# Attention and two mixture layers on one core: narrow matmuls in uninterrupted runs, and four buffers moved

## The chip, the core and the metric

The kernel runs on one core of a Trainium2 chip. The core has a matrix engine (TensorE, PE in the profile), three engines for elementwise work (VectorE or DVE, ScalarE or ACT, GpSimd or POOL) and SyncE (SP), which issues nearly all DMA transfers of this program, strictly in its own order. Every engine takes its instructions in the order in which they were written down when the program was built, and waits for other engines by semaphores. TensorE writes to PSUM, which has eight banks of 128 partitions. The metric is device time in microseconds (us).

## What is computed

```
attention: q, k, v of (4 batches, 8 heads, 576 tokens, 64)
    out_d  = softmax(mean4(q) @ mean4(k).T / 8) @ mean4(v)   # 144 tokens, each repeated 4 times
    out_l  = softmax over |i - j| < 4 of (q @ k.T / 8) @ v
    x      = (out_d + out_l) as (2304 tokens, 512)
first layer:  x = ((x @ w1) * (x @ w2)) @ w3 @ w_out         # w1, w2: 512x1024, w3: 1024x1024, w_out: 1024x512
second layer, 8 experts:
    e   = argmax(x @ w_gate);  p = softmax(x @ w_gate)[e]
    out = p * sigmoid((x @ w_output_gate)[e]) * (relu(x @ w1[e]) @ w2[e])
```

The weights of the first layer come as 64-bit floats; the kernel turns their bits into 32-bit ones with integer instructions on VectorE.

## The kernel before

A product of full precision is made of three matmuls (`mm3`, L390 to L392): each operand is split into a rounded part and a remainder, and high*high, high*low and low*high are summed in one PSUM bank. These are the wide matmuls: their output covers all 128 partitions, and they have 256, 272 or 384 columns here.

Order of the work. (1) Gate stage: for each eighth of `w_out`, `gate_step` loads it, converts it (`f64_bits`, L122, three VectorE instructions L127 to L129 through a PSUM bank), transposes it on TensorE (L318), copies the bank out on ScalarE (L320) and multiplies by the gate weights (L322). (2) w3 stage: `w3_part` converts w3 in 16 pieces, and `wc_half` makes the 16 halves of `wc` = w3 @ [w_out, gates] with 24 wide matmuls each (tile `w3T`), which `wc_out` brings to SBUF. (3) For each of six groups of 384 tokens (g = 0 to 5): the product stage `g1_step`, eight steps of 24 wide matmuls for (x @ w1) * (x @ w2), then `g2_step` with `wc` (tile `h`). In group 0, `w_parts` converts w1 and w2 beside the product stage, 16 pieces. (4) The experts, from about 482 us on; the change does not touch them.

Attention is laid beside (2) and (3). It has 16 units (a pair of heads of one batch), each with five steps that `step()` deals out by a table: `a_T`; `a_S1` with 24 local score matmuls (L191, output on 32 partitions, four of them side by side in the array) and three score matmuls on the means (L202); `a_S2`; `a_V1` with six transposes (L245); `a_V2` with 4 matmuls (L256) and 12 matmuls (L260), outputs on 64 partitions. L191, L256 and L260 are called narrow here. One record of the trace counts such a matmul twice ("x48" are 24 matmuls). Their banks are the three of the tag `at`.

What sets the order: the building tool orders each engine's list by priority, which is the place in the code; a step's instructions are raised by 120 places (`tc.high_priority(offset=120)`), and an instruction is taken once it is expected to be ready. Loads and buffers: a unit's `kz` (L160), `kc` (L153) and `v4` (L164) have one buffer each, so the next unit's load is issued when the last reader of the one before is done; the load of w1 and w2 pieces (tile `f`, L119, four buffers) is issued by `ahead()`. PSUM before: two banks `g1` (pool `ps1`), two `g2` (pool `ps2`), three `at`, one for conversions (`cv`, pool `psc`).

An uninterrupted run of narrow matmuls between wide ones is called an island below.

Of the kernel before, what the change touches and what calls it, by code (L numbers as in the profile page):

```python
# [20 lines left out]
P = 128  # L21
# [27 lines left out]
def attention_moe_kernel(ctx: ExitStack, tc: tile.TileContext, q, k, vw_in, v4_in, w1, w2, w3, w_out,  # L49
# [7 lines left out]
    psa = actx.enter_context(tc.tile_pool(name="psa", bufs=3, space=PSUM))  # L57
    psc = actx.enter_context(tc.tile_pool(name="psc", bufs=1, space=PSUM))
# [44 lines left out]
    staged = {}  # L103

# [3 lines left out]
    def f64_load(m, n):  # L108
        if m == "o":
            t = mt([P, 512], I64, "f64w", tag=f"W{n}")  # L110
            src = w_out[P * n:P * n + P, :]
        elif m == "3":
            t = mt([P, 512], I64, "f64w", tag=f"W{8 + n % 4}")
            src = w3[n]
        else:
            t = mt([P, 512], I64, "f64", tag=f"W{3 + 4 * m}") if n % 2 and n < 6 else mt([P, 512], I64, "f64", bufs=2)
            src = (w1, w2)[m][n]
        for c in pieces(m, n):
            nc.sync.dma_start(out=t[:, c], in_=src[:, c])  # L119
        staged[m, n] = t  # L120

    def f64_bits(t, dst):  # L122
        w = t.bitcast(U32).rearrange("p (n t) -> p n t", t=2)
        lo, hi = w[:, :, 0], w[:, :, 1]

        c = psc.tile([P, 512], F32, name="cv", tag="cv").bitcast(U32)[:, 0:dst.shape[-1]]
        nc.vector.tensor_scalar(c, hi, 3, 0x3FFFFFF8, op0=ALU.logical_shift_left, op1=ALU.bitwise_and)  # L127
        nc.vector.scalar_tensor_tensor(c, hi, 0xC0000000, c, op0=ALU.bitwise_and, op1=ALU.bitwise_or)
        nc.vector.scalar_tensor_tensor(dst, lo, 29, c, op0=ALU.logical_shift_right, op1=ALU.bitwise_or)  # L129
# [17 lines left out]
    st = {}  # L147

# [35 lines left out]
    def a_S1(u):  # L184
# [4 lines left out]
        for g in range(24):  # L189
            b, j = divmod(g, 4)  # L190
            nc.tensor.matmul(sl[32 * j:32 * j + 32, b], qT[:, 24 * g:24 * g + 32], kz[:, :, 24 * g:24 * g + 32],  # L191
                             start=True, stop=True, tile_position=(0, 32 * j))
# [8 lines left out]
        for qb in range(3):  # L201
            nc.tensor.matmul(sd[:, qb], qf[:, 96 * qb:96 * qb + 96], d["kd"], start=True, stop=True)  # L202
# [30 lines left out]
    def a_V1(u):  # L233
# [8 lines left out]
        for kb in range(2):  # L242
            pv = psa.tile([P, 512], F32, name="at", tag="at")
            for qb in range(3):
                nc.tensor.transpose(pv[0:72, 96 * qb:96 * qb + 96], ed[:, qb, 72 * kb:72 * kb + 72], ident[0:96, 0:96])  # L245
# [3 lines left out]
    def a_V2(u):  # L249
# [4 lines left out]
        for kb in range(2):  # L254
            for h in range(2):
                nc.tensor.matmul(xl[0][64 * h:64 * h + 64, 288:432], vd[:, kb, h, :], pt[:, kb, 144 * h:144 * h + 144],  # L256
                                 start=(kb == 0), stop=(kb == 1))
        for c in range(6):
            for h in range(2):
                nc.tensor.matmul(xl[c // 3][64 * h:64 * h + 64, 96 * (c % 3):96 * (c % 3) + 96], vw[:, c, D * h:D * h + D],  # L260
                                 bd[:, 2 * c + h, :], start=True, stop=True)
# [45 lines left out]
    def gate_step(f, gps, src):  # L307
        t = mt([P, DM], F32, "wf", tag=f"W{12 + f % 4}")
        for c in pieces("o", f):
            f64_bits(src[:, c], t[:, c].bitcast(U32))  # L310
# [26 lines left out]
    def w3_part(i, hf, w3T, src, wf3):  # L337
        t = wf3[:, (2 * i + hf) % 3, :]
        f64_bits(src, t.bitcast(U32))
# [19 lines left out]
    def w_part(m, f):  # L359
# [5 lines left out]
        f64_bits(src, t.bitcast(U32))  # L365
# [510 lines left out]
    for n in range(KF):  # L876
        if n == 1:
            nc.sync.dma_start(out=wg[:, :, 0:E], in_=w_gate.rearrange("(k p) e -> p k e", p=P))
            nc.sync.dma_start(out=wg[:, :, E:2 * E], in_=w_ogate.rearrange("(k p) e -> p k e", p=P))
# [26 lines left out]
    for i in range(KF):  # L906
        if i == KF - 2:
            ahead()
# [137 lines left out]
def _laid_out(inputs):  # L1046
# [18 lines left out]
    for n in ("moe_w1", "moe_w2"):  # L1065
        a[n] = _np.asarray(a[n]).reshape(KD, P, KF, P).transpose(2, 1, 0, 3).reshape(KF, P, 512)
    w = _np.asarray(a["moe2_w1"])
# [30 lines left out]
```

## Time and profile before

| what | value |
|---|---|
| median of 3 runs | 777.54 us (775.76 to 778.25) |
| the profiled execution's own time | 771.75 us |
| its span (first to last instruction) | 769.9 us |
| TensorE busy | 739.4 us, 96% of the span |
| VectorE busy | 436.3 us, 57% |
| ScalarE busy | 279.6 us, 36% |
| GpSimd busy | 322.9 us, 42% |
| mean granted TensorE clock | 0.989 of full speed |

Start times in a timeline are more telling than durations: matmuls overlap in the engine, so what one costs is the distance from its start to the next one's. Stages by the trace: gate stage to 28.67 us, w3 stage to 116.26 us, the product stage of group 0 to 168.06 us, and from there groups 0 to 5 until 482 us.

### The profile page before, as it was taken

Reading aid. Unit: us, or ns where it says so; the run is one execution under the profiler, and the core shown is the slowest. Engines: PE = TensorE matmul, PEld = TensorE weight load, DVE = VectorE, ACT = ScalarE, POOL = GpSimd, SP = SyncE. Lnnn points to the kernel's source line nnn. Section 1 sums busy time; section 2 is a strip of 40 time slices with the busy share of each in tenths; the row PEclk is TensorE's granted clock in tenths of the full one; section 3 lists DMA queues with packets and bytes.
Section 4 is the critical chain, followed back from the end, with each engine's and each line's share of the span. In section 5 each row is a group of like instructions: output and inputs, shape, how many; then the busy total and the mean of one; then the engine's idle time right before and its main releaser. Section 6 shows DMA issues by size and latency. Waiting matters only on the chain.

```text
span 769.9 us, 14699 instructions
## 1 busy us (share of the span) xinstructions
PE 739.4 (96%) x5710; PEld 683.3 (89%) x5711; DVE 436.3 (57%) x940; ACT 279.6 (36%) x624; POOL 322.9 (42%) x306
## 2 busy tenths in 40 slices
PE   5789999999999999999999999989999999999995
PEld 3667987888978898899899999978999999999994
DVE  8977897962653254445324343455765566676731
ACT  3423534550233223323421212045443644544610
POOL 6744576852360125213201112035654656755611
PEclk9899999999999999999999999998999999999999
DMA  9994565542131313121110010256645447447301
GB/s 325 332 240 139 173 189 160 171 136 91 54 109 31 115 29 111 47 77 38 42 42 22 1 42 1 60 199 241 213 146 210 148 149 268 146 148 260 111 23 39
DMA packets 38264, 97.72 MB, mean 127 GB/s; under 512 B 6018, under 2 KB 12930, under 8 KB 38192
## 3 DMA queue, kind: packets, MB, share of 16 engines
q1 hardware_dynamic: 34768, 86.82, 35.1%
q0 software_dynamic: 3424, 9.93, 3.6%
q8 instruction: 46, 0.75, 0.4%
q14 instruction: 26, 0.21, 0.1%
HBM read 84.93 MB, written 12.29 MB: 126 GB/s over the span
## 4 chain that ended last, share of the span: by engine, by line
PE 86%; issue 5%; POOL 3%; DVE 3%; DMA 1%; ACT 1%; SPq 0%; POOLq 0%; ACTq 0%
PE g L390 24%; PE g L392 24%; PE g L391 23%; PE at L260 3%; PE at L191 3%; PE at L256 2%; PE at L202 2%; PE tr L686 1%; PE at L245 1%; PE tr L779 1%; POOL out_dram L769 1%; DMA early<-in_moe_w_dram 1%; PE g L322 1%; POOL W L713 1%; DVE wf L129 1%
## 5 line engine op out<-in xcount | busy, mean ns | idle before, releaser
L390 PE MATMUL g<-xh,W 128*128 128x384 f32 x384 | 133.8, 349 | 0.0
L392 PE MATMUL g<-xh,W 128*128 128x384 f32 x384 | 131.0, 342 | 0.0
L391 PE MATMUL g<-xl,W 128*128 128x384 f32 x384 | 130.8, 341 | 0.0
L713 DVE TENSOR_TENSOR W<-raw,W 128x1024 fp32r<-128x1024 f32 x32 | 87.9, 2780 | 32.2 <-ACT W L711 30.1
L713 POOL TENSOR_TENSOR W<-raw,W 128x1024 fp32r<-128x1024 f32 x29 | 82.8, 2879 | 37.0 <-ACT W L711 37.0
L390 PE MATMUL g<-xT,W 128*128 128x288 f32 (+6 forms) x256 | 82.2, 321 | 1.0 <-ACT xT L690 1.0
L391 PE MATMUL g<-xT,W 128*128 128x288 f32 (+6 forms) x256 | 80.2, 313 | 0.0
L392 PE MATMUL g<-xT,W 128*128 128x288 f32 (+6 forms) x256 | 80.0, 312 | 0.0
L423 POOL TENSOR_TENSOR h<-a,h 128x384 fp32r<-128x384 f32 x30 | 30.7, 1023 | 113.9 <-ACT h L421 113.7
L390 PEld LDWEIGHTS g<-xh,W 128*128 128x128 f32 x384 | 72.2, 188 | 3.2 <-issue 0.4
L392 PEld LDWEIGHTS g<-xh,W 128*128 128x128 f32 x384 | 72.1, 188 | 1.9 <-issue 0.4
L391 PEld LDWEIGHTS g<-xl,W 128*128 128x128 f32 x384 | 72.2, 188 | 1.5 <-issue 0.2
L390 PE MATMUL g<-wc,h 128*128 128x272 f32 (+1 forms) x240 | 70.2, 293 | 0.0
L391 PE MATMUL g<-wc,h 128*128 128x272 f32 (+1 forms) x240 | 70.0, 292 | 0.0
L390 PE MATMUL g<-h,W 128*128 128x288 f32 (+5 forms) x224 | 70.0, 312 | 0.0
L392 PE MATMUL g<-wc,h 128*128 128x272 f32 (+1 forms) x240 | 69.9, 292 | 0.0
L391 PE MATMUL g<-h,W 128*128 128x288 f32 (+5 forms) x224 | 68.1, 304 | 0.0
L392 PE MATMUL g<-h,W 128*128 128x288 f32 (+5 forms) x224 | 68.1, 304 | 0.0
L711 ACT CAST W<-raw 128x1024 fp32r<-128x1024 f32 x61 | 59.8, 1046 | 8.1 <-DMA raw<-in_moe_w_dram 4.3
L419 DVE TENSOR_TENSOR a<-g,a 128x384 f32<-128x384 f32 x48 | 26.7, 556 | 60.2 <-PE g L392 56.4
L739 ACT ACTIVATE h<-g 128x288 fp32r<-128x288 f32 (+6 forms) x64 | 27.9, 436 | 78.6 <-PE g L392 76.3
L390 PEld LDWEIGHTS g<-xT,W 128*128 128x128 f32 x256 | 49.1, 192 | 1.5 <-ACT xT L690 1.4
(255 smaller groups left out, 1721.8 us busy)
## 6 DMA issues: line engine op xcount, KB each, us to landing
raw<-in_moe_w_dram SPq DMA_DIRECT2D x61, 512.0 KB, 3.6
f64w<-in_moe_w_dram SPq DMA_DIRECT2D x16, 512.0 KB
f<-in_moe_w_dram SPq DMA_DIRECT2D x16, 512.0 KB, 6.5
vw<-in_vw_dram SPq DMA_DIRECT2D x16, 384.0 KB, 3.2
kc<-in_k_dram SPq DMA_DIRECT2D x16, 288.0 KB, 6.4
qT<-in_q_dram SPq DMA_DIRECT2D x16, 288.0 KB, 4.3
kz<-in_k_dram SPq DMA_DIRECT2D x32, 144.0 KB, 3.7
v<-in_v_dram SPq DMA_DIRECT2D x16, 288.0 KB
```

What stands on the lines that cost most here:

```text
L191: nc.tensor.matmul(sl[32 * j:32 * j + 32, b], qT[:, 24 * g:24 * g + 32], kz[:, :, 24 * g:24 * g + 32], start=True, stop=True, tile_positio ...
L202: nc.tensor.matmul(sd[:, qb], qf[:, 96 * qb:96 * qb + 96], d["kd"], start=True, stop=True)
L256: nc.tensor.matmul(xl[0][64 * h:64 * h + 64, 288:432], vd[:, kb, h, :], pt[:, kb, 144 * h:144 * h + 144], start=(kb == 0), stop=(kb == 1))
L260: nc.tensor.matmul(xl[c // 3][64 * h:64 * h + 64, 96 * (c % 3):96 * (c % 3) + 96], vw[:, c, D * h:D * h + D], bd[:, 2 * c + h, :], start=T ...
L390: nc.tensor.matmul(ps, whi, xhi, start=first, stop=False)
L391: nc.tensor.matmul(ps, whi, xlo, start=False, stop=False)
L392: return nc.tensor.matmul(ps, wlo, xhi, start=False, stop=last)
L419: nc.vector.tensor_tensor(a, pp[1][:, 0:G], a, op=ALU.mult)
L423: eng.tensor_tensor(lo, a, hi.bitcast(F32), op=ALU.subtract)
L711: nc.scalar.copy(out=hi, in_=t)
L713: ins = eng.tensor_tensor(lo, t, hi.bitcast(F32), op=ALU.subtract)
L739: return nc.scalar.activation(out=t[:, 0, 0:C], in_=ps[:, 0:C], func=AF.Relu), nc.vector.scalar_tensor_tensor(t[:, 1, 0:C], ps[:, 0:C], 0. ...
```

## The change

The 24 matmuls of L191, the three of L202, each three of L245, and the 16 of L256 and L260 are each raised by 600 places (`burst`). The conversion bank is given up: `f64_bits` takes a `g1` bank in the gate and w3 stages and a `g2` bank for w1 and w2, and `at` has four banks in place of three. The first loads of w1 and w2 are queued on SyncE behind the last load of w3. The two gate weights are laid out on the host so that each partition's part is contiguous in DRAM. Lines after 145 stand some 4 to 8 lines further down in the changed file: L191 is L196, L245 is L252, L256 is L264, L260 is L268, L390 to L392 are L398 to L400.

```diff
-    psa = actx.enter_context(tc.tile_pool(name="psa", bufs=3, space=PSUM))
-    psc = actx.enter_context(tc.tile_pool(name="psc", bufs=1, space=PSUM))
+    psa = actx.enter_context(tc.tile_pool(name="psa", bufs=4, space=PSUM))
...
-            nc.sync.dma_start(out=t[:, c], in_=src[:, c])
+            f64_last[0] = nc.sync.dma_start(out=t[:, c], in_=src[:, c])
...
-    def f64_bits(t, dst):
+    def f64_bits(t, dst, ps, tag):
...
-        c = psc.tile([P, 512], F32, name="cv", tag="cv").bitcast(U32)[:, 0:dst.shape[-1]]
+        c = ps.tile([P, 512], F32, name=tag, tag=tag).bitcast(U32)[:, 0:dst.shape[-1]]
...
+    def burst():
+
+        return tc.high_priority(offset=600)
...
-        for g in range(24):
-            b, j = divmod(g, 4)
-            nc.tensor.matmul(sl[32 * j:32 * j + 32, b], qT[:, 24 * g:24 * g + 32], kz[:, :, 24 * g:24 * g + 32],
-                             start=True, stop=True, tile_position=(0, 32 * j))
+        with burst():
+            for g in range(24):
+                b, j = divmod(g, 4)
+                nc.tensor.matmul(sl[32 * j:32 * j + 32, b], qT[:, 24 * g:24 * g + 32], kz[:, :, 24 * g:24 * g + 32],
+                                 start=True, stop=True, tile_position=(0, 32 * j))
...
-            f64_bits(src[:, c], t[:, c].bitcast(U32))
+            f64_bits(src[:, c], t[:, c].bitcast(U32), ps1, "g1")
...
-        f64_bits(src, t.bitcast(U32))
+        f64_bits(src, t.bitcast(U32), ps1, "g1")
...
-        f64_bits(src, t.bitcast(U32))
+        f64_bits(src, t.bitcast(U32), ps2, "g2")
...
-            nc.sync.dma_start(out=wg[:, :, 0:E], in_=w_gate.rearrange("(k p) e -> p k e", p=P))
+            nc.sync.dma_start(out=wg[:, :, 0:E], in_=w_gate.rearrange("p (k e) -> p k e", e=E))
...
-            ahead()
+            with tc.issue_after(f64_last[0].ins):
+                ahead()
...
+    for n in ("moe2_w_gate", "moe2_w_output_gate"):
+        a[n] = _np.asarray(a[n]).reshape(KD, P, E).transpose(1, 0, 2).reshape(P, KD * E)
```

TensorE's order in the w3 stage before, where the second matmuls of the first unit meet a half of `wc` (`g_672`):

```order
L256 MATMUL at<-pt,vd 64x144
L390 MATMUL g_672<-wo,w3T 128x256
L256 MATMUL at<-pt,vd 64x144
L391 MATMUL g_672<-wc,w3T 128x256
L260 MATMUL at<-bd,vw 64x96
L392 MATMUL g_672<-wo,w3T 128x256
L260 MATMUL at<-bd,vw 64x96
L390 MATMUL g_672<-wo,w3T 128x256
```

The change, in the same stage, from one half of `wc` (`g_797`) to the next (`g_824`):

```order
L398 MATMUL g_797<-wo,w3T 128x256
L399 MATMUL g_797<-wc,w3T 128x256
L400 MATMUL g_797<-wo,w3T 128x256
L268 MATMUL at<-bd,vw 64x96 x12
L196 MATMUL at<-kz,qT_109 32x64 x3
L208 MATMUL at<-kd,qz 96x144
L196 MATMUL at<-kz,qT_109 32x64
L208 MATMUL at<-kd,qz 96x144
L196 MATMUL at<-kz,qT_109 32x64
L208 MATMUL at<-kd,qz 96x144
L196 MATMUL at<-kz,qT_109 32x64 x19
L398 MATMUL g_824<-wo,w3T 128x272
```

The twelve matmuls with `bd` now stand in one row between wide ones; the 24 with `kz` still share their place with three of the means, which are wide.

TensorE's order at the end of the gate stage and the start of the w3 stage before (`g_384`: last transposes of the gates; `g_442`, `g_469`: the first two halves of `wc`):

```order
L202 MATMUL at<-kd,qz 96x144 x2
L318 MATMUL g_324<-ident,wf 128x128 x4
L322 MATMUL g_161<-wot,wg 32x128 x8
L330 MATMUL g_384<-ident,gs 128x128 x2
L390 MATMUL g_442<-wo,w3T 128x256
L391 MATMUL g_442<-wc,w3T 128x256
L390 MATMUL g_469<-wo,w3T 128x272
L391 MATMUL g_469<-wo,w3T 128x272
L392 MATMUL g_442<-wo,w3T 128x256
```

The same place in the change (`g_381`, `g_439`, `g_466` are the same three; `qT_110` and `qT_109` belong to the second and the third unit):

```order
L196 MATMUL at<-kz,qT_110 32x64 x18
L208 MATMUL at<-kd,qz 96x144
L196 MATMUL at<-kz,qT_110 32x64 x6
L338 MATMUL g_381<-ident,gs 128x128 x2
L208 MATMUL at<-kd,qz 96x144 x2
L398 MATMUL g_439<-wo,w3T 128x256
L399 MATMUL g_439<-wc,w3T 128x256
L398 MATMUL g_466<-wo,w3T 128x272
L252 MATMUL at<-ident,ed 72x96 x6
L196 MATMUL at<-kz,qT_109 32x64 x24
L399 MATMUL g_466<-wo,w3T 128x272
L400 MATMUL g_439<-wo,w3T 128x256
```

The local scores of the second and the third unit now stand ahead of all but three of the first wide matmuls; before, the second unit's came after some 25 of them.

SyncE's order of loads before, from the first unit's values on (`f_1138` and so on are pieces of w1 and w2, `f64w` of w3):

```order
L164 DMA v_380<-in_v_dram 72x1024
L169 DMA vw<-in_vw_dram 128x768
L119 DMA f_1138<-in_moe_w_dram 128x512
L119 DMA f_1140<-in_moe_w_dram 128x512
L119 DMA f_1142<-in_moe_w_dram 128x512
L153 DMA kc<-in_k_dram 128x576
L160 DMA kz<-in_k_dram 64x576 x2
L154 DMA qT_112<-in_q_dram 128x576
L119 DMA f_1144<-in_moe_w_dram 128x512
```

The change, from the same load on, and further down where the pieces of w1 and w2 stand now:

```order
L168 DMA v_377<-in_v_dram 72x1024
L173 DMA vw<-in_vw_dram 128x768
L157 DMA kc<-in_k_dram 128x576
L164 DMA kz<-in_k_dram 64x576 x2
L158 DMA qT_109<-in_q_dram 128x576
L157 DMA kc<-in_k_dram 128x576
L164 DMA kz<-in_k_dram 64x576 x2
L168 DMA v_548<-in_v_dram 72x1024
L119 DMA f64w<-in_moe_w_dram 128x512
```

```order
L119 DMA f64w<-in_moe_w_dram 128x512 x4
L168 DMA v_1946<-in_v_dram 72x1024
L173 DMA vw<-in_vw_dram 128x768
L119 DMA f64w<-in_moe_w_dram 128x512 x2
L119 DMA f_1135<-in_moe_w_dram 128x512
L119 DMA f_1137<-in_moe_w_dram 128x512
L119 DMA f_1139<-in_moe_w_dram 128x512
L119 DMA f_1141<-in_moe_w_dram 128x512
L164 DMA kz<-in_k_dram 64x576 x2
```

Four loads of w1 and w2 have left the front of the queue; they stand behind w3's last piece.

## Rows read from the trace of the kernel before

**Rows 1.** Stretches: start:end, length, busy us (instructions) per engine, granted clock, DMA.
```profile
0.00:28.67 28.67, 17.40 (x152) 12.66 (x154) 25.73 (x58) 12.42 (x27) 20.80 (x42) 1.00 0.95 335
28.67:116.26 87.59, 81.01 (x785) 70.85 (x786) 73.01 (x155) 36.25 (x98) 48.76 (x55) 0.96 0.68 197
116.26:168.06 51.80, 51.80 (x441) 42.98 (x440) 42.34 (x85) 27.52 (x72) 36.77 (x38) 1.00 0.55 164
168.06:242.28 74.22, 74.22 (x614) 63.85 (x614) 32.24 (x97) 21.83 (x63) 24.91 (x32) 1.00 0.26 79
242.28:318.08 75.80, 75.80 (x623) 66.51 (x623) 32.70 (x102) 24.14 (x67) 24.15 (x30) 1.00 0.27 79
318.08:386.73 68.65, 68.65 (x570) 63.24 (x569) 29.66 (x90) 22.29 (x61) 15.42 (x18) 1.00 0.14 44
```

**Rows 2.** PE timeline, wide matmuls of 256 columns alone: start, length, line, operation.
```profile
52.72 0.28 PE L391 MATMUL g<-wc,w3T 128*128 128x256 f32 x1
53.31 0.28 PE L390 MATMUL g<-wo,w3T 128*128 128x256 f32 x1
```

**Rows 3.** PE timeline, narrow matmuls of L260 one by one among wide ones.
```profile
57.27 0.38 PE L390 MATMUL g<-wo,w3T 128*128 128x256 f32 x1
63.50 0.44 PE L245 MATMUL at<-ident,ed 96*72 96x96 f32 x3
```

**Rows 4.** PE timeline, L260 in one run, then wide matmuls of 384 columns.
```profile
285.81 1.16 PE L260 MATMUL at<-bd,vw 128*64 128x96 f32 x24
286.91 0.44 PE L390 MATMUL g<-xh,W 128*128 128x384 f32 x1
...
287.36 0.34 PE L392 MATMUL g<-xh,W 128*128 128x384 f32 x1
288.06 0.34 PE L390 MATMUL g<-xh,W 128*128 128x384 f32 x1
```

**Rows 5.** PE timeline, L191: 24 in one run, and one by one.
```profile
48.31 0.88 PE L191 MATMUL at<-kz,qT 128*32 128x64 f32 x48 [0.26 <-ACT w3T L341]
...
70.09 0.30 PE L191 MATMUL at<-kz,qT 128*32 128x64 f32 x2
73.90 0.30 PE L191 MATMUL at<-kz,qT 128*32 128x64 f32 x2
```

**Rows 6.** VectorE timeline: a reduction that waited for its load, and the next.
```profile
43.37 0.75 DVE L181 TENSOR_REDUCE kd<-kc 128x144 f32<-128x576 f32 x1 [0.55 <-DMA kc<-in_k_dram]
44.10 0.41 DVE L355 TENSOR_TENSOR wc<-g,wc 128x256 fp32r<-128x256 f32 x1
```

**Rows 7.** What PE waited for, us in total, times, longest.
```profile
PE g L390 <- DVE wc L355: 4.1, 2, 2.8
PE g L392 <- POOL w3T L343: 2.1, 1, 2.1
PE g L390 <- ACT w3T L341: 1.1, 1, 1.1
```

**Rows 8.** DMA issues of kz in the first 60 us: KB, us to landing.
```profile
kz<-in_k_dram SPq DMA_DIRECT2D x8, 144.0 KB, 9.0
```

**Rows 9.** The same from 60 to 330 us.
```profile
kz<-in_k_dram SPq DMA_DIRECT2D x24, 144.0 KB, 3.2
```

**Rows 10.** ScalarE timeline: the copy out of a bank of transposes.
```profile
13.34 0.59 ACT L320 COPY wot<-g 128x512 f32<-128x512 f32 x1 [0.68 <-PE g L318]
```

**Rows 11.** VectorE timeline: the conversion that begins behind it.
```profile
14.22 0.69 DVE L127 TENSOR_SCALAR cv<-f64w 128x512 uint32<-128x512 uint32 x1
```

**Rows 12.** VectorE groups of the first 170 us: count, busy us, mean ns.
```profile
L127 DVE TENSOR_SCALAR cv<-f 128x512 uint32<-128x512 uint32 x16 | 10.9, 684 | 0.2
L419 DVE TENSOR_TENSOR a<-g,a 128x384 f32<-128x384 f32 x8 | 4.4, 554 | 2.4 <-PE g L392 2.3 <-ACT a L418 0.2
```

**Rows 13.** Two more stretches, columns as in rows 1.
```profile
31.58:36.10 4.52, 4.52 (x21) 4.52 (x21) 4.28 (x12) 0.51 (x1) 2.10 (x3) 0.51 1.03 337
285.00:297.00 12.00, 12.00 (x161) 11.15 (x160) 4.32 (x12) 4.95 (x12) 5.91 (x8) 1.00 0.22 61
```

More of the change, by code (lines that the diff above doesn't have):

```diff
@@ L103, in attention_moe_kernel @@
     staged = {}
+    f64_last = [None]
     def pieces(m, n):
@@ L200, in a_S1 @@
         qf = qz.rearrange("p h n -> p (h n)")
-        for qb in range(3):
-            nc.tensor.matmul(sd[:, qb], qf[:, 96 * qb:96 * qb + 96], d["kd"], start=True, stop=True)
+        with burst():
+            for qb in range(3):
+                nc.tensor.matmul(sd[:, qb], qf[:, 96 * qb:96 * qb + 96], d["kd"], start=True, stop=True)
         ed = at([96, 3, 144], F32, "ed", bufs=2)
@@ L243, in a_V1 @@
             pv = psa.tile([P, 512], F32, name="at", tag="at")
-            for qb in range(3):
-                nc.tensor.transpose(pv[0:72, 96 * qb:96 * qb + 96], ed[:, qb, 72 * kb:72 * kb + 72], ident[0:96, 0:96])
+            with burst():
+                for qb in range(3):
+                    nc.tensor.transpose(pv[0:72, 96 * qb:96 * qb + 96], ed[:, qb, 72 * kb:72 * kb + 72], ident[0:96, 0:96])
             nc.scalar.copy(out=pt[:, kb], in_=pv[0:72, 0:288])
@@ L253, in a_V2 @@
         xl = [psa.tile([P, 512], F32, name="at", tag="at") for _ in range(2)]
[L254 to L261, printed above, removed]
+        with burst():
+            for kb in range(2):
+                for h in range(2):
+                    nc.tensor.matmul(xl[0][64 * h:64 * h + 64, 288:432], vd[:, kb, h, :], pt[:, kb, 144 * h:144 * h + 144],
+                                     start=(kb == 0), stop=(kb == 1))
+            for c in range(6):
+                for h in range(2):
+                    nc.tensor.matmul(xl[c // 3][64 * h:64 * h + 64, 96 * (c % 3):96 * (c % 3) + 96], vw[:, c, D * h:D * h + D],
+                                     bd[:, 2 * c + h, :], start=True, stop=True)
         up = at([P, 144], F32, "up")
@@ L877, in attention_moe_kernel @@
         if n == 1:
-            nc.sync.dma_start(out=wg[:, :, 0:E], in_=w_gate.rearrange("(k p) e -> p k e", p=P))
-            nc.sync.dma_start(out=wg[:, :, E:2 * E], in_=w_ogate.rearrange("(k p) e -> p k e", p=P))
+            nc.sync.dma_start(out=wg[:, :, 0:E], in_=w_gate.rearrange("p (k e) -> p k e", e=E))
+            nc.sync.dma_start(out=wg[:, :, E:2 * E], in_=w_ogate.rearrange("p (k e) -> p k e", e=E))
         f64_load("o", n)
```

## The prediction

> **What bounds the kernel now.** I read the busy time of the engines in stretches first, because shares over the whole span mix stages. From 116 to 387 us TensorE has no idle time at all, while VectorE is busy for 42.3 of 51.8 us in the product stage of group 0 and for less than half of the time after it [rows 1]. So there the end is set by how fast TensorE gets through its list. In the first 116 us it idles for 11.3 + 6.6 us, and VectorE is busy for 98.7 of 116.3 us; two engines share the bound there. Next I read TensorE's timeline by the distance between starts, because "busy" hides what a matmul costs its neighbours. Six wide matmuls of 256 columns alone start within 0.59 us, five distances, 0.118 us each [rows 2]. Between 57.27 and 63.50 us ten wide ones alternate with ten of L260: 6.23 us, 0.623 us a pair [rows 3]. The same L260 in one run: 12 matmuls in 1.10 us, 0.092 us each [rows 4]. So a lone L260 costs 0.623 - 0.118 - 0.092 = 0.413 us more than its work. L191 alone: seven pairs in 3.81 us, 0.544 us a pair [rows 5]; 24 in one run take no more than 0.88 us, 0.037 each; the excess is 0.544 - 0.118 - 0.037 = 0.39 us. That is the price of an island, whatever its length: TensorE loses it on the way in and out.
>
> **The change part by part.** *Islands.* I counted them in the order of both programs. Before there are 149, 80 with 64-partition outputs and 69 with 32; in the change there are 66, 28 and 38 (the three L202 are wide and still stand inside L191, so many of its runs stay split). 52 x 0.413 + 31 x 0.39 = 21.5 + 12.1 = 33.6 us less. L256 alone I price like L260. By place: up to the end of the product stage of group 0, 65 become 34 (31 less, 12.5 us); behind it 84 become 32 (52 less, 21.1 us). Behind 168 us TensorE has no idle time that could hide this [rows 1], so that part should arrive whole.
>
> *Attention earlier.* In the change the product stage of group 0 holds no attention matmul, and three more units stand in the w3 stage. That moves work; it adds none. It is safe if VectorE keeps up. Up to 168.06 us it is busy for 25.7 + 73.0 + 42.3 = 141.1 us [rows 1], and the change's list up to the same point holds the same conversions and reductions; 168.1 - 12.5 = 155.6 us leave it 14.5 us of slack, where it now has 27. In the product stage 12 conversions remain, 12 x 3 x 0.684 = 24.6 us, and 8 x 0.554 = 4.4 us of L419 [rows 12], 29.0 us against 192 wide matmuls of 384 columns at 0.175 us (four in 0.70 us [rows 4]), 33.6 us. TensorE stays the bound by 4.6 us. I take nothing for it; if the conversions start late, the gap behind it is up to 5 us.
>
> *w1 and w2 loads behind w3's.* Four loads of 512 KB leave the crowded first 50 us. There a kz load takes 9.0 us from issue to landing, later 3.2 [rows 8, 9]. One wait on the path hangs on this: TensorE waits 2.8 us for L355 [rows 7], which stands on VectorE behind a reduction that began at 43.37 us, when its kc load landed [rows 6]. I take that wait as gone, -2.8 us. The pieces are wanted only at the end of the w3 stage, and w3's last piece is loaded four pieces ahead of its own conversion (four buffers), so a landing of some us is in time there; 0.
>
> *A new wait.* The second and third units' L191 now stand with only about 1.6 us of TensorE work between them, ahead of nearly all wide matmuls. Both read the single kz buffer, so the third unit's load is issued when the second's L191 is done: two issues, 1.1 us, and a landing of 3.2 to 9.0 us [rows 8, 9]. TensorE then stands for 2.7 to 8.5 us, with the whole w3 stage queued behind it, and VectorE waits for the scores. In the same place it now waits 2.1 + 1.1 us for the parts of w3T [rows 7], and those waits pass beneath the new one. Net -0.5 to +5.3 us; the four loads ahead are gone, so I go near the lower end, +1.5 us.
>
> *Conversion banks.* A conversion in the gate stage needs a bank that the transposes used before. The copy that frees it runs from 13.34 to 13.93 us and the next conversion starts at 14.22 [rows 10, 11]: 0.29 us of margin per eighth, nothing if it holds, eight times 0.6 us at most if it fails. I take 0. The `g2` banks are idle while w1 and w2 are converted, since TensorE's product stage uses only `g1`; 0. The fourth `at` bank frees no wait that the profile shows; 0. The gate loads are two issues on a queue that nobody waits for at that point; 0, and some tenths of a us either way.
>
> Sum: -33.6 - 2.8 + 1.5 = -34.9 us against the profiled execution's own 771.75 us (769.9 of span and 1.85 around it). That execution lies 5.8 us under the median of the three runs, 777.54 us; against the median the sum gives 742.6, so **743 us**.
>
> **The rivals.** *VectorE takes over.* The w3 stage gets three more units of reductions; if VectorE needs the 27 us of slack that it has now, because its waits come from handing work to and fro and not from load, nothing is gained before 168 us, and 21.1 us remain: 777.5 - 21.1 = 756 us. For it: 98.7 of the first 116.3 us are busy. Against it: some of its waits are for loads [rows 6], which get faster.
>
> *The clock falls.* [...] If the bursts of four units that stand together between the last four halves of wc kept the clock down, some 26 us of TensorE work (96 wide ones at 0.122 and four units at 3.5 us, an estimate) would take twice as long: 743 + 26 = 769 us. Against it: from 285 to 297 us two such bursts and twelve transposes passed at a granted clock of 1.00 [rows 13]. [...]
>
> *Bursts starve TensorE (slower).* Raised by 600, a burst is placed as soon as it is expected to be ready, and TensorE can't pass it. If each unit's L191 waited for its kz, 1.1 us of issue and 3.2 us of landing with nothing in between, 15 units would cost 64 us. It decides from 34.9 / 15 = 2.3 us a unit; at 3.5 us the time is 777.5 - 34.9 + 52.5 = 795 us. Against it: apart from the pair above, the order puts at least 4.5 us of TensorE work (at the prices above) between one unit's L191 and the next, more than 1.1 + 3.2; before, where it is little more than 5 us in places, no wait of TensorE for kz is among the large ones [rows 7].
>
> **How the numbers follow.** The forecast has 0.70, VectorE 0.18, the clock 0.06, starving 0.05, anything else 0.01. The forecast's own range is 735 (the islands' partners in the array add a few us) to 751; with VectorE's case and the margins above, 733 to 763 leaves out the clock and starving. Differences under 0.3% (2.3 us) can't be told from none; the first three cases are all faster, a mixture of new waits could end near zero: faster 0.93, same 0.02, slower 0.05.
>
> **What would show it.** Right: no pairs at 0.54 or 0.62 us in TensorE's timeline, group 0's product stage with starts 0.175 us apart throughout, the stages behind it shorter by about 21 us together, one wait of a few us before the first wide matmuls. Wrong: idle time of TensorE before L400 or L390's successors in the w3 stage with VectorE at full load (first rival), a granted clock of 0.5 there (second), TensorE waiting for kz, `ed` or `pt` at many places (third). If islands are gone and the time is not, the price per island was a price of something else, and the reading of rows 3 and 5 is wrong.

## The result and the profile after

The changed kernel takes 751.61 us (median of 4 runs, 750.13 to 756.41), the kernel before 777.43 us (775.76 to 778.25): a ratio of 0.9681, 95% interval 0.9633 to 0.9730. That is 25.8 us less where 34.4 less were forecast. The profiled execution took 750.13 us (span 748.3, 21.6 less than before). The spans differ by less than the medians because the profiled execution of before lies 5.7 us under its median and that of the change 1.5 us under its own; all views by stage are of the profiled executions.

The first view is the stretches of the kernel after, cut at the same places of the work as [rows 1]: start of `wc`, end of `wc`, first output stage (where `g2_step` of group 0 begins), and two groups behind it (columns: length, busy us of PE, PEld, DVE, ACT and POOL with counts, granted clock, DMA share, GB/s).

```profile
0.00:37.58 37.58, 24.41 (x206) 16.79 (x208) 29.27 (x62) 12.92 (x27) 24.71 (x48) 0.99 0.78 264
37.58:131.25 93.67, 86.80 (x980) 77.72 (x980) 83.56 (x183) 47.47 (x139) 58.25 (x64) 0.93 0.69 209
131.25:171.21 39.96, 37.38 (x228) 34.79 (x226) 32.62 (x56) 16.85 (x33) 31.63 (x29) 1.00 0.54 177
171.21:238.46 67.25, 66.69 (x640) 62.41 (x640) 34.04 (x104) 24.55 (x71) 22.03 (x28) 1.00 0.30 92
238.46:300.88 62.42, 62.41 (x586) 60.15 (x586) 30.05 (x94) 20.22 (x55) 21.74 (x28) 1.00 0.26 76
```

Against [rows 1] there are two different outcomes. The gate stage is 8.9 us longer (37.58 against 28.67). From there to the first output stage 133.6 us stand against 139.4, only 5.8 less, at a lower granted clock (0.93 in the w3 stage against 0.96). Behind it the next three groups are shorter (67.3, 62.4 and 64.9 us against 74.2, 75.8 and 68.7); the rest up to the last output group, which holds no attention, is equal (95.2). The last output group begins 289.8 us after the first, before 313.9: 24.1 us less. The rest, the experts, is 0.7 us shorter (287.3 against 288.0). Sum: 8.9 - 5.8 - 24.1 - 0.7 = -21.7, the 21.6 of the spans but for rounding.

Next, TensorE's timeline of the kernel after at one run of L264 and L268 (L256 and L260 of before), with what follows it.

```profile
273.76 0.71 PE L264 MATMUL at<-pt,vd 72*64 72x144 f32 x8
274.30 1.16 PE L268 MATMUL at<-bd,vw 128*64 128x96 f32 x24
275.39 0.44 PE L252 MATMUL at<-ident,ed 96*72 96x96 f32 x3
```

All sixteen matmuls of a unit's `a_V2` (32 passes in the count) are done in 1.63 us, the distance from 273.76 to 275.39; the pairs of [rows 3] are gone here. L196 (L191 of before) is not whole. The same view further ahead:

```profile
213.48 0.31 PE L196 MATMUL at<-kz,qT 128*32 128x64 f32 x6
213.72 0.49 PE L208 MATMUL at<-kd,qz 128*96 128x144 f32 x2
214.13 0.30 PE L196 MATMUL at<-kz,qT 128*32 128x64 f32 x2
214.36 0.49 PE L208 MATMUL at<-kd,qz 128*96 128x144 f32 x2
214.78 0.30 PE L196 MATMUL at<-kz,qT 128*32 128x64 f32 x2
215.01 0.49 PE L208 MATMUL at<-kd,qz 128*96 128x144 f32 x2
215.43 0.76 PE L196 MATMUL at<-kz,qT 128*32 128x64 f32 x38
216.12 0.60 PE L252 MATMUL at<-ident,ed 96*72 96x96 f32 x5
```

The three wide L208 stand inside the run, as the prediction said they would: four islands, 2.64 us.

Now the gate stage, where the 8.9 us were lost. TensorE's timeline of the kernel after (the brackets give idle time just before, and what ended it):

```profile
12.16 1.91 PE L330 MATMUL g<-wot,wg 128*32 128x128 f32 x8 [0.68 <-ACT wot L328]
14.01 1.12 PE L326 MATMUL g<-ident,wf 128*128 128x128 f32 x4
15.86 1.91 PE L330 MATMUL g<-wot,wg 128*32 128x128 f32 x8 [0.73 <-ACT wot L328]
17.70 1.11 PE L326 MATMUL g<-ident,wf 128*128 128x128 f32 x4
19.55 1.92 PE L330 MATMUL g<-wot,wg 128*32 128x128 f32 x8 [0.73 <-ACT wot L328]
```

And of the kernel before (L318 are the transposes, L322 the gate matmuls):

```profile
12.15 1.09 PE L318 MATMUL g<-ident,wf 128*128 128x128 f32 x4 [0.81 <-DVE wf L129]
13.17 2.65 PE L322 MATMUL g<-wot,wg 128*32 128x128 f32 x16
15.75 0.66 PE L318 MATMUL g<-ident,wf 128*128 128x128 f32 x4
17.14 1.06 PE L322 MATMUL g<-wot,wg 128*32 128x128 f32 x8 [0.73 <-ACT wot L320]
```

The gate matmuls of one eighth (four; "x8" counts each twice) take 1.91 us in the one and 1.06 us in the other, four transposes 1.11 and 0.66. An eighth takes 3.69 us (15.86 to 19.55) against 2.38 (from 17.14 to the next run at 19.52). Both wait 0.73 us for the copy in these eighths. What before has and after has not is a long stretch without a wait, from 12.15 to 16.4 us, with the gate matmuls of two eighths in one piece; within it the speed rises, and it stays up through the waits that follow. The kernel after gets there only at about 26 us, when the scores of the first unit stand where it waited before. The trace's records of the granted clock fit this: the first one, 1.00, begins at 15.6 us before and at 26.5 us after, and for the time ahead of it there is none. In the kernel after, conversions and transposes share the two `g1` banks, and the transposes of the third eighth stand behind the gate matmuls of the second in TensorE's list, so that pair is gone. VectorE was held up there as well, for 5.04 us, by the copy out of a `g1` bank. The first conversion of w3, which the first `wc` needs, comes later too: the second row is of the kernel after, the third of the kernel before (VectorE's timelines):

```profile
26.92 0.70 DVE L127 TENSOR_SCALAR g<-f64w 128x512 uint32<-128x512 uint32 x1 [5.04 <-ACT wot L328]
34.41 0.68 DVE L127 TENSOR_SCALAR g<-f64w 128x512 uint32<-128x512 uint32 x1
24.21 0.69 DVE L127 TENSOR_SCALAR cv<-f64w 128x512 uint32<-128x512 uint32 x1
```

So the stage lost time in two places. TensorE's last gate matmul ends at 32.9 us, before at 26.6, which is 6.3 us later. From there to the first `wc` it takes 4.7 us, before 2.1: the second unit's scores stand there, and then a wait of 2.54 us for w3T, whose conversion VectorE began 10.2 us later than before.

Last, the start of the w3 stage in the kernel after, TensorE's timeline:

```profile
37.58 0.58 PE L398 MATMUL g<-wo,w3T 128*128 128x256 f32 x1 [2.54 <-ACT w3T L349]
...
38.40 1.16 PE L252 MATMUL at<-ident,ed 96*72 96x96 f32 x6
39.49 1.51 PE L196 MATMUL at<-kz,qT 128*32 128x64 f32 x48
```

After a stand of 2.54 us the 24 L196 take 1.51 us, at a granted clock of 0.50; at 1.00 they take 0.88, as L191 in [rows 5]. In the stretch from 38 to 46 us the granted clock was 0.65 in the mean, 0.50 up to 43 us and 1.00 from 43.6 us on:

```profile
38.00:46.00 8.00, 8.00 (x99) 7.36 (x100) 8.00 (x26) 4.47 (x14) 6.42 (x8) 0.65 0.80 249
```

The two other falls of the clock ahead of the first output stage, both to 0.50, came behind stands of TensorE as well, of 2.04 and 1.75 us:

```profile
90.67 0.39 PE L398 MATMUL g<-wo,w3T 128*128 128x272 f32 x1 [2.04 <-DVE wc L363]
118.03 1.61 PE L268 MATMUL at<-bd,vw 128*64 128x96 f32 x24 [1.75 <-DMA vw<-in_vw_dram]
```

```profile
91.40:94.80 3.40, 3.40 (x18) 3.40 (x17) 3.40 (x8) 0.12 (x1) 0.91 (x1) 0.50 1.05 294
118.70:122.10 3.40, 3.40 (x26) 3.18 (x22) 0.98 (x3) 1.36 (x7) 2.74 (x3) 0.50 0.89 276
```

A stand alone doesn't decide it: the kernel before stood for 2.8 us up to 44.6 us [rows 7], and its granted clock was 1.00 from 36.1 us to its first output stage.

### The profile page after: what moved, and what is told of

Its sections match the earlier page's. It is cut to its first block, busy times and chain, and to the rows that moved or that the text cites. A ratio compares the mean times of both kernels' runs of the same rounds, so it can differ in the third digit from the quotient of the medians.

```text
span 748.3 us, 14713 instructions
## 1 busy us (share of the span) xinstructions
PE 711.9 (95%) x5710; PEld 674.6 (90%) x5711; DVE 438.3 (59%) x940; ACT 279.5 (37%) x624; POOL 326.0 (44%) x306
## 4 chain that ended last, share of the span: by engine, by line
PE 77%; DVE 8%; issue 5%; DMA 4%; POOL 4%; ACT 1%; SPq 0%; POOLq 0%; DVEq 0%; ACTq 0%
PE g L398 22%; PE g L400 22%; PE g L399 22%; PE at L268 2%; PE at L196 1%; PE at L208 1%; DVE g L128 1%; PE tr L694 1%; PE tr L787 1%; PE g L330 1%; DVE g L127 1%; PE at L264 1%; POOL W L377 1%; DMA vw<-in_vw_dram 1%; DVE wf L129 1%
## 5 line engine op out<-in xcount | busy, mean ns | idle before, releaser
L398 PE MATMUL g<-xh,W 128*128 128x384 f32 x384 | 131.4, 342 | 0.9 <-DVE a L427 0.5
L400 PE MATMUL g<-xh,W 128*128 128x384 f32 x384 | 129.9, 339 | 1.7 <-POOL W L377 1.4
L399 PE MATMUL g<-xl,W 128*128 128x384 f32 x384 | 128.9, 336 | 0.0
L721 DVE TENSOR_TENSOR W<-raw,W 128x1024 fp32r<-128x1024 f32 x32 | 87.9, 2781 | 32.9 <-ACT W L719 24.1
L398 PE MATMUL g<-xT,W 128*128 128x288 f32 (+6 forms) x256 | 81.5, 318 | 1.0 <-ACT xT L698 1.0
L400 PE MATMUL g<-xT,W 128*128 128x288 f32 (+6 forms) x256 | 79.4, 310 | 0.0
L400 PEld LDWEIGHTS g<-xh,W 128*128 128x128 f32 x384 | 72.1, 188 | 3.3 <-POOL W L377 3.0
L398 PEld LDWEIGHTS g<-xh,W 128*128 128x128 f32 x384 | 72.2, 188 | 3.1 <-issue 1.1
L398 PE MATMUL g<-h,W 128*128 128x288 f32 (+5 forms) x224 | 69.9, 312 | 0.0
L400 PE MATMUL g<-h,W 128*128 128x288 f32 (+5 forms) x224 | 68.0, 303 | 0.0
L399 PE MATMUL g<-wc,h 128*128 128x272 f32 (+1 forms) x240 | 67.9, 284 | 0.0
L398 PE MATMUL g<-wc,h 128*128 128x272 f32 (+1 forms) x240 | 67.7, 284 | 0.0
L400 PE MATMUL g<-wc,h 128*128 128x272 f32 (+1 forms) x240 | 67.6, 284 | 0.0
L427 DVE TENSOR_TENSOR a<-g,a 128x384 f32<-128x384 f32 x48 | 26.6, 555 | 55.3 <-PE g L400 53.3
L777 POOL DMA_INDIRECT out_dram<-orow,b_si x24 | 23.5, 978 | 62.8 <-DVE orow L776 59.3
## 6 DMA issues: line engine op xcount, KB each, us to landing
kc<-in_k_dram SPq DMA_DIRECT2D x16, 288.0 KB
qT<-in_q_dram SPq DMA_DIRECT2D x16, 288.0 KB
v<-in_v_dram SPq DMA_DIRECT2D x16, 288.0 KB
```

The source lines that it names most:

```text
L398: nc.tensor.matmul(ps, whi, xhi, start=first, stop=False)
L399: nc.tensor.matmul(ps, whi, xlo, start=False, stop=False)
L400: return nc.tensor.matmul(ps, wlo, xhi, start=False, stop=last)
L427: nc.vector.tensor_tensor(a, pp[1][:, 0:G], a, op=ALU.mult)
L721: ins = eng.tensor_tensor(lo, t, hi.bitcast(F32), op=ALU.subtract)
L777: ins = nc.gpsimd.indirect_dma_start(out=out, out_offset=bass.IndirectOffsetOnAxis(ap=rt["si"][0:n, r, b:b + 1], axis=0), in_=t[0:n], in_o ...
```

## The experiments

Two theories were set against each other first: the bursts give what was forecast and another part of the change takes it back in the gate and w3 stages; or VectorE's load holds everything up to the first output stage. Times are medians; the kernel before was timed beside each group, at 774 to 779 us.

Islands are counted in the programs; where a run of L268 passes straight into one of L196 it counts as two.

| kernel | us (lowest to highest) | ratio to before, interval | islands ahead + behind | `wc` begins | first output stage | from there to the last group's | granted clock from `wc` to there |
|---|---|---|---|---|---|---|---|
| before | 777.43 | | 65 + 84 | 28.7 | 168.1 | 313.9 | 0.98 |
| after | 751.61 (750.13 to 756.41) | 0.9681 [0.9633, 0.9730] | 34 + 32 | 37.6 | 171.2 | 289.8 | 0.95 |
| own bank | 745.37 (741.52 to 746.44) | 0.9586 [0.9523, 0.9648] | 35 + 34 | 28.1 | 165.2 | 291.0 | 0.96 |
| bursts only | 744.70 (743.30 to 744.92) | 0.9589 [0.9532, 0.9647] | 28 + 34 | 29.9 | 164.9 | 290.5 | 0.95 |
| no bursts | 769.29 (765.58 to 774.81) | 0.9922 [0.9885, 0.9958] | 46 + 80 | 38.3 | 169.7 | 311.8 | 0.98 |
| gate in `at` | 749.53 (747.17 to 753.42) | 0.9646 [0.9582, 0.9709] | 36 + 32 | 28.2 | 173.7 | 289.8 | 0.92 |
| less VectorE | 744.37 (743.81 to 745.33) | 0.96 [0.9537, 0.9663] | 32 + 34 | 27.3 | 164.8 | 290.5 | 0.96 |
| L197 whole | 742.74 (739.39 to 743.76) | 0.9561 [0.9492, 0.9631] | 24 + 19 | 28.3 | 167.2 | 285.5 | 0.94 |
| fill | 747.95 (747.16 to 751.66) | 0.9646 [0.9549, 0.9742] | 43 + 32 | 36.3 | 167.5 | 290.3 | 0.97 |
| fill, L196 whole | 751.04 (750.56 to 754.99) | 0.9693 [0.9597, 0.9788] | 22 + 19 | 33.8 | 174.4 | 285.2 | 0.94 |
| bursts only, L197 whole | 739.48 (739.02 to 739.90) | 0.9526 [0.9439, 0.9612] | 17 + 19 | 29.2 | 164.2 | 285.8 | 0.96 |
| own bank, L197 whole, fill | 736.69 (735.48 to 739.16) | 0.9501 [0.9412, 0.9591] | 18 + 19 | 28.5 | 160.8 | 285.4 | 0.99 |
| fill once | 747.51 (745.47 to 749.74) | 0.9628 [0.9557, 0.9698] | 34 + 32 | 33.9 | 164.5 | 289.8 | 0.99 |

**Own bank.** The change without its part on conversion banks.

```
-    psa = ...(name="psa", bufs=4, space=PSUM)
+    psa = ...(name="psa", bufs=3, space=PSUM);  psc = ...(name="psc", bufs=1, space=PSUM)
-    f64_bits(..., ps1, "g1")  # and ps2, "g2"
+    f64_bits(..., psc, "cv")
```

> The change without its bank part: conversions have their own bank again, attention three; bursts, late loads and gate layout stay. Its order has 69 islands (66 in the change). Theory: the gate stage grew from 28.7 to 37.6 us because conversions and transposes share two banks, so that each eighth's transposes wait behind the gate matmuls of the eighth before and TensorE stays slow; without it the first wide matmul comes at about 29 us and the time is 751.6 - 9 = 743 us. Rival (the loads or the raised bursts delay the start): the first wide matmul stays at 36 us or later and the time is about 751 us.

Measured 745.4 us, near the theory: the part on banks costs 6.2 us, and the two kernels' runs do not overlap. The gate stage has its pair again, TensorE's timeline:

```profile
12.84 1.08 PE L327 MATMUL g<-ident,wf 128*128 128x128 f32 x4 [1.16 <-DVE wf L130]
13.85 2.77 PE L331 MATMUL g<-wot,wg 128*32 128x128 f32 x16
17.94 1.06 PE L331 MATMUL g<-wot,wg 128*32 128x128 f32 x8 [0.73 <-ACT wot L329]
```

**Bursts only.** The kernel before, with `with tc.high_priority(offset=600)` around L191, L202, L245 and L256 to L260 and nothing else of the change.

> Before, with the raised bursts alone. 62 islands against 149: at 0.40 us each 35 us less, 742 us, if the price of an island is what the distances between starts say. Rival (VectorE is the bound up to the second product stage whatever the order): only the 50 islands behind group 0's product stage count, 20 us, 757 us.

Measured 744.7 us: the bursts alone are worth all that the change with its own bank is worth. The later loads of w1 and w2 and the gates' layout add nothing that can be measured (745.4 against 744.7).

**No bursts.** The change with `burst()` returning an empty context.

> The change without the 600 places of priority; banks, loads and gate layout stay. 126 islands against 149 before. Theory: 23 islands less, 9 us, against 9 us lost in the gate stage: about 777 us, so that the bursts make all of the gain. Rival (the banks and the late loads make part of the gain): 765 us or less.

Measured 769.3 us, between the two. It has the slow gate stage (`wc` begins at 38.3 us), and from there to the first output stage it takes 131.4 us, 8.0 less than before, with 19 islands fewer. Part of the 8.0 is moved work: 59 L196 stand ahead of the first `wc`, before 24. So the order of the attention moves with the buffers too, and islands go without any burst.

**Gate in `at`.** In the gate stage alone the conversions take an attention bank: `f64_bits(..., psa, "at")`.

> The change with one edit: the conversions of the gate stage alone take attention's four banks in place of the two of the transposes. 68 islands. Theory (the shared pair of banks in the gate stage is what cost 9 us): first wide matmul at 29 to 31 us, 743 us. Rival (attention, short of banks at the start, is late instead): no gain, 750 us or more.

Measured 749.5 us, against the theory (its profiled execution was the slowest of four, 753.4). The gate stage is repaired (28.2 us), but the next 145.5 us are 11.9 longer than in the kernel after, at a granted clock of 0.92 and with new waits. What TensorE waited for longest from `wc` to the first output stage (us in total, times, longest):

```profile
PE at L196 <- DMA kz<-in_k_dram: 4.2, 2, 2.7
PE g L400 <- POOL W L377: 3.1, 2, 2.4
PE at L252 <- POOL ed L231: 2.4, 1, 2.4
```

This made the second question: what holds the stretch from `wc` to the first output stage.

**Less VectorE.** On top of the own bank, the conversions of w3, w1 and w2 without their third instruction.

```
-        nc.vector.scalar_tensor_tensor(c, hi, 0xC0000000, c, ...)
+        nc.vector.scalar_tensor_tensor(dst if short else c, hi, 0xC0000000, c, ...)
+        if short: return
```

> The changed kernel with the conversions' own bank back, in which the conversions of w3, w1 and w2 leave out their third VectorE instruction, so that these weights lose the lowest three bits of their fractions: 32 x 0.68 = 21.9 us less VectorE work, all of it between the first wide matmul of wc (28 us) and the output stage of group 0 (165.2 us in the kernel with the bank alone). Islands as there (32 + 34 against 35 + 34). Theory, VectorE's load holds this stretch: the output stage begins 8 to 15 us earlier, 150 to 157 us, and the time is 731 to 738 us. Rival, TensorE's own list and clock hold it: the stage begins no more than 3 us earlier, the time is 742 to 746 us.

VectorE's theory falls. Stretches from `wc` to the first output stage, first with the own bank, then with less VectorE work:

```profile
28.05:165.21 137.16, 124.79 (x1260) 112.36 (x1261) 120.86 (x248) 66.80 (x179) 93.82 (x101) 0.96 0.66 202
```

```profile
27.31:164.84 137.53, 126.35 (x1276) 113.27 (x1277) 101.74 (x217) 66.41 (x181) 94.09 (x102) 0.96 0.65 203
```

VectorE is busy 19.1 us less and the stretch is 0.4 us longer. So VectorE's load does not set this length. TensorE is busy for 125 and 126 of the 137 us; the rest are waits, and part of the busy time is at a clock under 1.00 (0.96 in the mean of both stretches).

**L197 whole.** On top of the own bank, the three wide L208 (L202 of before) are no longer raised.

```
-        with burst():
+        with ExitStack():
             for qb in range(3): nc.tensor.matmul(sd[:, qb], ...)
```

> The changed kernel with the conversions' own bank back, in which the three wide L208 are no longer raised, so that they leave the runs of L197 whole: 43 islands instead of 69, 11 fewer before the output stage of group 0 and 15 fewer behind. Theory, an island costs 0.4 to 0.46 us wherever it stands: behind the output stage's begin 6 to 7 us less, before it up to 4.5 us less, 734 to 740 us. Rival, the pooled scores now come late and TensorE waits for the exponentials: behind it less than 3 us won, waits of TensorE for ed or pt of 1 us and more, 743 to 750 us.

Measured 742.7 us, a little above the theory and a little under the rival; its runs and those of the kernel with the bank alone overlap. A unit's scores in TensorE's timeline:

```profile
202.22 0.88 PE L197 MATMUL at<-kz,qT 128*32 128x64 f32 x48
203.03 0.98 PE L209 MATMUL at<-kd,qz 128*96 128x144 f32 x6
203.75 0.43 PE L399 MATMUL g<-xh,W 128*128 128x384 f32 x1
```

The same 27 matmuls took 2.64 us in four islands of the kernel after and take 1.53 us in one: 0.37 us for each island less. Behind the first output stage the whole is 5.4 us for 15 islands, 0.36 each. Ahead of it nothing came: 11 islands fewer, and the output stage 2.0 us later, at a clock of 0.94. There the rival's sign is seen: TensorE waits once for `ed`, for 2.7 us.

**Fill.** In every eighth of the gate stage four more transposes, into a bank that nobody reads, stand where TensorE waits for the copy. It ran twice.

```
+        fill = psa.tile([P, 512], F32, name="at", tag="at")
+        for n in range(KD):
+            nc.tensor.transpose(fill[:, P * n:P * n + P], t[:, P * n:P * n + P], ident)
         wot = ...
```

> The changed kernel with four more transposes per eighth of the gate stage, into an attention bank that nobody reads, between the four transposes and the eight gate matmuls that wait 0.73 us for ACT's copy; the result is the same. Theory, the gate stage runs at half speed because TensorE stood before every run: with the gap filled the speed doubles in the first eighths, a run of eight gate matmuls falls from 1.91 to about 1.0 us and an eighth from 3.69 to less than 3.0 us, although it holds more work; wc begins by 33 us. Rival, the time of an eighth is the chain itself and the filler only adds to it: the runs stay at 1.9 us, an eighth takes 3.7 to 4.2 us, wc begins at 37.6 us or later.

> The kernel with the filling transposes once more, timed (one time of 746.5 us so far). Theory, the higher clock in the gate stage is worth what the one run showed: 744 to 748 us, 4 to 7 us under the changed kernel's 751.6, with the output stage of group 0 beginning by 167 us. Rival, the one time was chance: 749 to 752 us.

TensorE's timeline in the first of the two runs (L329 is the filler, L333 the gate matmuls):

```profile
15.50 1.06 PE L333 MATMUL g<-wot,wg 128*32 128x128 f32 x8 [0.30 <-ACT wot L331]
16.50 0.66 PE L326 MATMUL g<-ident,wf 128*128 128x128 f32 x4
16.99 0.60 PE L329 MATMUL at<-ident,wf 128*128 128x128 f32 x4
17.88 1.06 PE L333 MATMUL g<-wot,wg 128*32 128x128 f32 x8 [0.29 <-ACT wot L331]
```

An eighth takes 2.38 us with more work in it, instead of 3.69. One line of the first expectation failed: `wc` begins at 36.3 in the second run, not by 33. The gates end there at 31.4 us; behind them stand the second unit's scores, which wait 1.3 us for `kz`, and six transposes (L252). The output stage came at 167.5 us, not by 167 as the second expectation has it. The times were 746.5 and 747.95 us; its runs and those of the kernel after overlap (747.16 to 751.66, 750.13 to 756.41), so the gain of 3.7 us in the medians is not certain.

**Fill once.** The filler in the second eighth alone (`if f == 1:` ahead of it); the rest of TensorE's list is that of the kernel after, row by row.

> The changed kernel with four filling transposes in one eighth of the gate stage alone, the second, between its transposes and its gate matmuls; apart from these four, TensorE's list is that of the changed kernel. Theory, one stretch without a wait early on is all that the kernel before had and the changed one lacks (12.15 to 16.4 us): after it the runs of eight gate matmuls fall from 1.91 to about 1.06 us and stay there although each later eighth waits 0.73 us again; five eighths at 2.38 instead of 3.69 us, wc begins at 30 to 33 us instead of 37.6, and the time is 744 to 749 us. Rival, each gap by itself keeps the speed down, so only the second eighth changes: the later runs stay at 1.91 us, an eighth at 3.69 us, wc begins at 37 us or later, 750 to 753 us.

The theory holds for the gate stage. TensorE's timeline (L330 filler, L334 gate matmuls):

```profile
8.12 1.91 PE L334 MATMUL g<-wot,wg 128*32 128x128 f32 x8 [0.68 <-ACT wot L332]
10.40 1.09 PE L326 MATMUL g<-ident,wf 128*128 128x128 f32 x4 [0.37 <-DVE tok L99]
11.28 1.06 PE L330 MATMUL at<-ident,wf 128*128 128x128 f32 x4
12.27 1.17 PE L334 MATMUL g<-wot,wg 128*32 128x128 f32 x8
...
14.77 1.06 PE L334 MATMUL g<-wot,wg 128*32 128x128 f32 x8 [0.73 <-ACT wot L332]
```

Up to the filler, at 11.28 us, every row of TensorE stands where it stood in the kernel after. The filler of 1.06 us closes one gap; the gate matmuls behind it take 1.17 us, and all later runs that are whole take 1.06 us instead of 1.91, though those at 14.77, 17.15 and 19.52 us wait 0.73 us again. The last gate matmul ends at 28.2 us instead of 32.9, and the clock stays at 0.99 up to the first output stage, which begins at 164.5 instead of 171.2 us. The median is 747.5, 4.1 us under the kernel after, and the runs do not overlap, though the intervals of the two ratios do. `wc` began later than expected (33.9), behind waits of 1.9 us for `kz` and 1.5 us for w3T: of the 8.9 us that the change lost up to `wc`, the speed of the gates gives back 3.7. The third unit's wait for `kz`, which the prediction expected, is seen here as well, 1.2 us at 36.2 us; the kernel after has none.

**Three combinations**, to see whether the gains add up.

> The kernel with the filling transposes, in which the three wide L211 are no longer raised either: 41 islands, 22 before the output stage of group 0 and 19 behind, instead of 43 and 32. Theory, an island behind the output stage's begin is worth what the kernel with whole runs showed, 0.36 us: 13 x 0.36 = 4.7 us less there; the 21 before it are worth anything from nothing (what they win is lost again to standing and a lower clock) to 0.36 us each: 734 to 742 us. Rival, islands were not what the whole runs won: 745 to 748 us.

Both fell: 751.0 us is above the rival's range too. Behind the output stage the gain is there (285.2), ahead of it 7 us are lost. The stretch from the end of `wc` to 140 us, here and in the kernel with the filler alone:

```profile
117.64:140.00 22.36, 13.21 (x72) 10.51 (x71) 15.99 (x36) 9.70 (x26) 9.27 (x10) 0.72 0.57 170
```

```profile
120.81:140.00 19.19, 14.90 (x117) 12.99 (x115) 15.54 (x32) 9.31 (x22) 14.04 (x16) 0.91 0.68 202
```

TensorE is busy for 13.2 of 22.4 us, at a clock of 0.72, and no engine is full. Its longest waits there are 3.1 us for VectorE's `a` (L430), 2.0 us for GpSimd's `W` (L380) and 1.9 us for the load of `vw`; what held these is not shown.

> The kernel before with the raised bursts alone, in which the three wide L208 are not raised: 36 islands, 17 before the output stage of group 0 and 19 behind, instead of 28 and 34. Theory, behind it 15 x 0.36 = 5.4 us less, before it 0 to 4 us less: 735 to 740 us. Rival, before it as much is lost to standing as behind it is won, as the kernel with whole runs and the loads late showed in part: 742 to 745 us.

Measured 739.5 us, as the theory had it, and a range of less than 1 us.

> The kernel with whole L197 runs (742.7 us), with the filling transposes in its gate stage, where the conversions have their own bank: 37 islands, 18 + 19, instead of 24 + 19. Theory, the filler raises TensorE's speed in the gate stage and after it less time is lost to a low clock: the output stage of group 0 begins by 164 us instead of 167.2, and the time is 736 to 740 us. Rival, this gate stage reaches full speed by 18 us anyway, and 32 transposes more cost up to 8 x 0.6 = 4.8 us or nothing: 742 to 748 us.

Measured 736.7 us, the fastest of all, 14.9 us under the kernel after. The stretch from `wc` on, without the filler and with it:

```profile
28.25:167.24 138.99, 124.74 (x1261) 114.31 (x1261) 121.36 (x248) 66.20 (x179) 93.55 (x101) 0.94 0.64 199
```

```profile
28.54:160.80 132.26, 116.92 (x1261) 108.65 (x1261) 119.25 (x248) 66.01 (x179) 91.16 (x99) 0.99 0.68 209
```

The filler did not shorten its own stage (28.25 and 28.54), yet the next is 6.7 us shorter at a clock of 0.99. The time lost to the clock, length times what is missing to 1, was 8.3 us and is 1.3. Why the clock holds there isn't settled: TensorE idles as long in both (14.3 and 15.3 us), and the filler also moved the order of the w3 stage (24 islands ahead became 18).

## Why the prediction was right, and where it was wrong

The time lies in the range and the sign is right; the cause was the one named, and it gave what it was priced at where nothing else moved. But 751.6 lies just above the forecast's own 735 to 751 and is covered by the margin for VectorE's case; three other terms were missed, and the islands behind the output stage gave 3.0 us more than forecast. That the sum comes within 8.6 us of the measured time is in part luck.

*Islands behind the first output stage: right.* Forecast -21.1 us for 52, measured -24.1. Of these about 1.6 us is moved work: the trace has eight units' L268 ahead of the first output stage where before it had seven units' L260, and a unit's `a_V2` takes 1.63 us. That leaves 22.5 / 52 = 0.43 us an island, forecast 0.40 to 0.41. The other kernels give 0.43 (own bank), 0.44 (bursts only), and 0.36 for the split L197.

*Islands ahead of it: the step that failed.* The prediction put 31 islands and -12.5 us here, and with the loads and the new wait -13.8. Measured is +3.1, 16.9 us apart. From `wc` to the output stage it was -5.8, 8.0 short. Time lost to the clock went from 0.04 x 87.6 = 3.5 to 0.07 x 93.7 = 6.6 us, all of it in the w3 stage, 3.1 more; TensorE's idle time went from 6.6 to 9.4 us, 2.9 more where 1.3 less was forecast, 4.2 apart. That makes 7.3 of the 8.0; the moved work nearly cancels (one unit's `a_V2` comes in, 1.6 us, and the scores of about one unit went out into the gate stage, about 1.2). So the islands did go, and TensorE got through its list sooner; it then stood at other engines' results, and ran slower after it had stood (a granted clock of 0.50, the 24 L196 in 1.51 us instead of 0.88). The own bank, with a quick gate stage, shows the same: 30 islands fewer ahead, and from `wc` to the output stage 137.2 us against 139.4.

*Conversion banks: wrong, and the other 8.9 us.* The prediction asked only whether a conversion finds its bank free, and bounded the loss by 8 x 0.6 = 4.8 us; one conversion alone waited 5.04 us. It did not look at TensorE's list, in which a pair of transposes comes apart, nor at VectorE's, in which the first conversion of w3 goes from 24.2 to 34.4 us (24.8 with the own bank). Of the 8.9 us, 6.3 lie ahead of the last gate matmul and 2.6 behind it. Fill once shows that ahead of it most of the loss is the speed, and not the waits as such: the same waits with one gap closed keep the higher speed, and the gates end 4.7 us earlier. For `wc` that is worth 3.7 us; the other 5.2 stay with the shared banks, and the own bank wins back all of it. That the shared banks took the pair away is shown by the own bank (28.1 us) and the gate in `at` (28.2); which of the two banks held what is argued only.

*Loads late, -2.8 us: wrong.* Bursts only, without late loads, has 1.0 us of VectorE's wait for `kc` where before had 4.6, and the same time as the own bank with them. TensorE's wait for VectorE's `wc`, which the term took as gone, was 4.1 us in all before [rows 7] and is 4.0 us after. The new wait for `kz`, +1.5: TensorE stood 2.54 us ahead of the first `wc`, but for w3T. *Gate layout, fourth bank: 0*, as far as the own bank and bursts only can tell.

*The rivals.* VectorE taking over gave 756 us, and nothing gained ahead of the output stage was its mark; that mark came true, but less VectorE shows that its load is not the reason. The clock falling was priced for bursts that follow one another; it fell after waits instead, to 0.50, for some 13 us in all ahead of the output stage, and not in the groups behind it (1.00 from 171.21 to 482 us). The doubling can be worked out from the 0.51 of [rows 13]; that bursts keep the clock down, no run shows: the one at 273.76 us, with transposes next to it, passed at 1.00. Starving: no wait for `kz` among the large ones of the kernel after.

*Not shown.* In fill once four 32-bit transposes in one gap, beside the gate matmuls, were followed by 1.06 us in place of 1.91 for the gate matmuls of the rest of the stage; whether four matmuls there would have done as much, no run shows. An island cost 0.36 to 0.44 us in these runs; what TensorE does in that time is not shown either, and the prediction's "on the way in and out" is its author's reading.

What stays open: why the clock from `wc` on differs between kernels whose lists differ little (0.92 to 0.99), and with it up to 9 us ahead of the output stage. Every kernel at 0.96 or less has waits of TensorE of 1 us and more there, but so have the two at 0.99 (3.1 us for `wc` with own bank, whole L197 and fill; 1.2 us for `kz` with fill once).

## What to carry to other kernels

Count the changes between narrow and wide matmuls in TensorE's list and price them from one pair and one run in the trace (0.39 and 0.41 us here); where TensorE had no idle time that price arrived whole (0.43 us an island), and where it waited for others most of it was given back (8.0 of 13.8 us between `wc` and the first output stage). When a buffer is shared between a conversion and a transpose, look at what becomes of TensorE's order, above all at places where it works for some us without a wait (from 12.15 to 16.4 us here). A gap in a stage that runs at the lower speed may be worth filling with work that nobody needs: here four transposes of 1.06 us in one gap brought `wc` forward by 3.7 us.

## What the runs showed of the hardware that was not expected

TensorE's speed in the gate stage depended on what had gone before. With waits of about 0.7 us it took 1.91 us for an eighth's gate matmuls in five runs of the kernel after (8.12 to 25.1 us); with the same waits it took 1.06 us once the speed had risen within a stretch without a wait (before: 12.15 to 16.4 us; fill once: 10.40 to about 14.0 us). How much work that takes the runs don't settle: the kernel after also works from 12.16 to 15.1 us without a wait, and stays slow. The granted clock of a view doesn't show this first stage: it says 0.99 for the stretch from 0 to 37.58 us, although the durations are nearly double there, because the trace has no record of the clock ahead of 26.5 us. That a lower clock stood there too is an estimate from the durations: 1.91 to 1.06 us is a ratio of 1.8, and the 24 L196 at a recorded clock of 0.50 take 1.51 us against 0.88 at 1.00, a ratio of 1.7. The durations change near the first record: before, four transposes take 1.09 us at 12.15 and 0.66 at 15.75 us (record at 15.6); after, they take 1.12 us at 25.09, and the 24 L196 behind them 1.04 at 26.13 us (record at 26.5).

More work made a stage shorter: 32 transposes more brought an eighth from 3.69 to 2.38 us, and four more brought the first output stage from 171.2 to 164.5 us.
